# Rotary embedding on GpSimd in five instructions a tensor instead of nine

## The chip, the cores and the metric

The kernel runs on one core of a Trainium2 chip. The metric is the device time of one execution in microseconds. Five engines work side by side, each through its own list of instructions in order: TensorE (PE; its weight loads are shown apart as PEld), VectorE (DVE), ScalarE (ACT), GpSimd (POOL) and SyncE (SP), which issues most DMAs. They wait for one another by semaphores alone.

## The reference

Attention with rotary embedding over 4 batches, 8 heads, 576 positions and a head size of 64, followed by a gated feed-forward network with a convolution of three taps along the positions (512 to 1024 to 512 channels).

```python
def rotate(x):                                   # q and k
    x1, x2 = (x[..., :half], x[..., half:])
    return np.concatenate([x1 * cos - x2 * sin, x1 * sin + x2 * cos], axis=-1)
scores = scale * np.matmul(q_rot, k_rot.transpose(0, 1, 3, 2))
attn = np.exp(scores - max); attn = attn / (sum + 1e-09)
x = np.matmul(attn, v)                           # heads side by side: 512 channels
h = np.maximum(x @ w_in, 0.0)
conv_out = sum of conv_w[k] * h shifted by k - 1 positions
out = (h * sigmoid(conv_out)) @ w_out
```

## The kernel before

Two heads of one batch make a pair; there are 16 pairs. A pair takes five steps, one for each piece of 128 (the last: 64) query positions of both heads. In a step TensorE makes the scores (`sp`, L261), VectorE takes their negated maximum (`negm`, L269), ScalarE the exponential with its sum (`st`, or `str` in the last step, L273), TensorE turns the result (`tp`, L321) and ScalarE copies it out (`pt`, L199). The product with v (L389), the division by the sums (rinv, L366 to L368, and `xn`, L403) and a split of the result into a high and a low part (L406 on ScalarE, L410 on GpSimd) follow a pair later.

Beside this, the first 26 steps convert the weights of the feed-forward network, which arrive as 64-bit numbers, in pieces of 512 columns: four instructions on VectorE for each piece (L569, L575, L580, L585), a copy on ScalarE (L635) and four subtractions of 128 columns on GpSimd (L632). From step 26 on (`WIDE`) the feed-forward network itself runs between the attention steps: matmuls (L431), relu (L439), convolution on VectorE (L447, L449), tanh on ScalarE (L455), the gate (L458), a split (L466, L467), and the second product (L540, in the tail L520). After the last pair the feed-forward network goes on alone (the tail).

The rope of the pairs 1 to 15 is done by `rope` (L186 to L193) on GpSimd, once for q and once for k. The tensor `rq` or `rk` lies as 128 partitions by 18 blocks of 2 x 32 numbers. A multiplication with a table, in place (L190), covers all 1152 columns, and an addition of the second 32 numbers of each block to the first 32, in place (L193), writes 576. VectorE then turns the sums into `qT` (L234) and `kT` (L237), after which SyncE's queue loads the next pair into the same buffer (L149 to L151). Pair 0 goes another way (`rope0`, L164 to L184).

The order on every engine is written out by hand: a plan (`at(n, rank, fn)`) gives each piece of work a step and a rank in it, and inside an engine the instructions run in the order in which the plan calls them. For a pair that begins at step n, `rope` stands at step n - 6 (later pairs: n - 8 for q, n - 7 for k) with rank 18, which is at the end of a step; the transposes follow one to four steps later.

Of the kernel before, what the change touches and what calls it, by code (L numbers as in the profile page):

```python
# [12 lines left out]
ALU = mybir.AluOpType  # L13
# [7 lines left out]
def attention_moe_kernel(ctx, tc, q, k, v, w_in, conv_w, w_out, tab, tabx, out):  # L21
    nc = tc.nc
# [35 lines left out]
    tabt = keep.tile([128, S // 32, 2, 32], F32, name="tabt")  # L58
# [126 lines left out]

    def rope(p, part):  # L186
        x = raw[p, part]
        for a in range(0, 18, 3):
            y = x[:, a:a + 3]
            nc.gpsimd.tensor_tensor(out=y, in0=y, in1=tabt[:, a:a + 3], op=ALU.mult)  # L190
        for a in range(0, 18, 6):
            y = x[:, a:a + 6]
            nc.gpsimd.tensor_tensor(out=y[:, :, 0, :], in0=y[:, :, 0, :], in1=y[:, :, 1, :], op=ALU.add)  # L193

    QT, KT = {}, {}
# [502 lines left out]
    def emit():  # L698
        with tc.manual_schedule(engines=engines):
# [18 lines left out]
            for p in range(1, NP):  # L718
                n = STEPS * p
                early = n - 10 >= WIDE - 1  # L720
                for i, part in enumerate("qk"):
                    if p > 1:
                        at(max(n - 10, WIDE) if early else n - 9 + 2 * i, 19.6 if early else 19, lambda p=p, part=part: load(p, part))
                    at(n - 8 + i if early else max(n - 6, 0), 18, lambda p=p, part=part: rope(p, part))
                    at(n - 5 + i * (n - 15 < WIDE) if early else max(n - 4 + 2 * i, 2), 0.45, lambda p=p, part=part: emit_TQ(p, part))
                at(n + 1, 19, lambda p=p: load_v(p))
# [144 lines left out]
```

## Time and profile before

| What | Value |
|---|---|
| Three runs | 481.36, 483.17 and 483.62 us, median 483.17 |
| The profiled execution | span 480.6 us, 12404 instructions; the profile gives no other time for it |
| TensorE | 450.5 us busy (94%) |
| VectorE | 359.5 us busy (75%), 640 instructions |
| ScalarE | 331.9 us busy (69%) |
| GpSimd | 304.5 us busy (63%), 487 instructions |
| Granted TensorE clock | 0.996 of full speed over the span |

The busy shares are means over stages that differ: weights are converted up to some 160 us, the attention and the feed-forward network run together up to some 390 us, and the rest is feed-forward alone. A busy time counts an instruction from its start to its end, with whatever it waits for in between. The rows below take the stages apart.

### The profile page before, as it was taken

What the parts mean: (1) busy time and instruction counts of PE and PEld (TensorE: products, weight loads), DVE (VectorE), ACT (ScalarE), POOL (GpSimd) and SP (SyncE); (2) the same over time, 40 slices, a digit from 0 to 9 for tenths busy, and PEclk for the clock granted to TensorE, in tenths of its full rate; (3) what the DMA queues carried; (4) which work ended last, traced back from release to release, by engine and by line L of the source; (5) the groups of instructions that cost most, each with busy time, mean ns of one, the idle gap of its engine ahead of it and who ended that gap; (6) DMA issues with size and microseconds to landing.
All of it is one profiled execution on the core that took longest, in us unless ns stands there. A gap on an engine that the chain in (4) does not pass through costs nothing.

```text
span 480.6 us, 12404 instructions
## 1 busy us (share of the span) xinstructions
PE 450.5 (94%) x4572; PEld 355.8 (74%) x4572; DVE 359.5 (75%) x640; ACT 331.9 (69%) x951; POOL 304.5 (63%) x487
## 2 busy tenths in 40 slices
PE   1879887988999999999999999999999999999997
PEld 1446554656767787979788887879787978899886
DVE  5599899996898987777868686866874656467921
ACT  1699787887879786868778686867695953245510
POOL 3869999999797979393929394756530313144510
PEclk9999999899999999999999999999999999999999
DMA  9985877856436070718153362518020100100011
GB/s 186 245 138 158 175 179 143 152 117 161 74 81 142 9 149 25 137 37 134 39 99 74 78 95 60 103 40 145 9 66 16 49 13 25 46 22 23 0 67 44
DMA packets 140559, 42.71 MB, mean 89 GB/s; under 512 B 132156, under 2 KB 135252, under 8 KB 140500
## 3 DMA queue, kind: packets, MB, share of 16 engines
q1 hardware_dynamic: 139156, 41.54, 41.0%
q8 instruction: 36, 0.59, 0.5%
q10 hardware_dynamic: 1344, 0.39, 0.4%
q14 instruction: 23, 0.19, 0.1%
HBM read 37.12 MB, written 4.79 MB: 87 GB/s over the span
## 4 chain that ended last, share of the span: by engine, by line
PE 69%; DVE 9%; DMA 7%; SPq 7%; ACT 5%; issue 2%; POOL 0%; DVEq 0%; POOLq 0%
PE pm L431 13%; PE pm L540 11%; PE sp L261 11%; PE pm L389 11%; PE mt L520 10%; PE mt L431 7%; PE tp L321 5%; DVE negm L269 2%; DMA rd<-rt 2%; SPq L150 2%; DMA rq<-q 2%; ACT st L273 1%; ACT pt L199 1%; SPq L151 1%; DVE c L449 1%
## 5 line engine op out<-in xcount | busy, mean ns | idle before, releaser
L269 DVE TENSOR_REDUCE negm<-sp 128x1 f32<-128x576 f32 x144 | 102.5, 748 | 32.7 <-PE sp L261 24.1
L273 ACT ACTIVATE st<-sp,negm 128x576 f32<-128x576 f32 x128 | 93.7, 739 | 31.1 <-DVE negm L269 30.1
L261 PE MATMUL sp<-kT,qT 64*128 64x288 f32 (+4 forms) x556 | 98.7, 458 | 3.1 <-ACT st L273 1.3
L199 ACT ACTIVATE pt<-tp 128x512 f32<-128x512 f32 (+3 forms) x176 | 84.3, 532 | 3.7 <-PE tp L321 3.3
L449 DVE SCALAR_TENSOR_TENSOR c<-rr,cw,c 128x288 f32<-128x288 f32 x128 | 80.6, 629 | 4.2
L467 POOL TENSOR_TENSOR gm<-c,gm 128x288 fp32r<-128x288 f32 (+4 forms) x72 | 44.7, 626 | 49.7 <-ACT gm L466 49.7
L431 PE MATMUL pm<-xT,winh 128*128 128x290 f32 x352 | 74.5, 305 | 0.0
L190 POOL TENSOR_TENSOR rq<-rq,tabt 128x192 f32<-128x192 f32 x90 | 59.9, 698 | 11.7 <-DMA rq<-q 8.7
L410 POOL TENSOR_TENSOR xT<-xn,xT 128x290 fp32r<-128x290 f32 x32 | 29.5, 923 | 58.0 <-ACT xT L406 57.9
L261 PEld LDWEIGHTS sp<-kT,qT 64*128 64x128 f32 (+1 forms) x556 | 46.3, 176 | 24.2 <-issue 9.1
L321 PEld LDWEIGHTS tp<-idf,st 64*128 64x128 f32 x1024 | 42.6, 140 | 25.7 <-ACT st L273 12.9
L190 POOL TENSOR_TENSOR rk<-rk,tabt 128x192 f32<-128x192 f32 x90 | 56.9, 665 | 1.5 <-DMA rk<-k 1.1
L321 PE MATMUL tp<-idf,st 64*128 64x64 f32 x1024 | 49.4, 228 | 9.1 <-ACT st L273 7.3
L431 PEld LDWEIGHTS pm<-xT,winh 128*128 128x128 f32 x352 | 56.2, 189 | 1.8
L431 PE MATMUL pm<-xT,winl 128*128 128x290 f32 x176 | 52.0, 295 | 0.0
L389 PE MATMUL pm<-pt,vm 128*64 128x290 f32 x368 | 49.8, 411 | 0.4 <-ACT pt L199 0.4
L540 PE MATMUL pm<-wouth,gm 64*128 64x256 f32 x512 | 49.3, 281 | 0.0
L458 DVE SCALAR_TENSOR_TENSOR c<-c,rr 128x288 f32<-128x288 f32 x64 | 38.6, 624 | 10.4 <-ACT c L455 10.4
L540 PEld LDWEIGHTS pm<-wouth,gm 64*128 64x128 f32 x512 | 41.9, 185 | 0.0
L447 DVE TENSOR_SCALAR c<-rr,cw 128x288 f32<-128x288 f32 x56 | 24.9, 444 | 20.4 <-ACT rr L439 20.0
L389 PEld LDWEIGHTS pm<-pt,vm 128*64 128x64 f32 x368 | 25.6, 136 | 17.6 <-ACT pt L199 1.1
L540 PE MATMUL pm<-woutl,gm 64*128 64x256 f32 x256 | 37.7, 276 | 0.0
(118 smaller groups left out, 907.2 us busy)
## 6 DMA issues: line engine op xcount, KB each, us to landing
rq<-q SPq DMA_DIRECT2D x30, 144.0 KB
rq<-q SPq DMA_DIRECT2D x60, 72.0 KB
rk<-k SPq DMA_DIRECT2D x30, 144.0 KB
rk<-k SPq DMA_DIRECT2D x60, 72.0 KB
w<-moe_w_in SPq DMA_DIRECT2D x8, 512.0 KB
vm<-v SPq DMA_DIRECT2D x32, 128.0 KB
w<-moe_w_out SPq DMA_DIRECT2D x8, 512.0 KB
rb<-rd SPq DMA_DIRECT2D x16, 144.0 KB
```

Source lines behind the costliest of these rows:

```text
L190: nc.gpsimd.tensor_tensor(out=y, in0=y, in1=tabt[:, a:a + 3], op=ALU.mult)
L199: nc.scalar.activation(out=out, in_=in_, func=AF.Copy, scale=1.0 if sc is None else sc)
L261: nc.tensor.matmul(out=out, lhsT=qt[64 * h:64 * h + 64, c], rhs=kt[64 * h:64 * h + 64, a:a + n], start=True, stop=True)
L269: reds.setdefault((p, s), []).append(lambda: nc.vector.tensor_reduce(out=nm, in_=sc, axis=AX.XY if len(sc.shape) == 3 else AX.X, op=ALU.ma ...
L273: lambda: nc.scalar.activation(out=dst, in_=sc, func=AF.Exp, bias=nm, scale=1.0, accum_out=sm)
L321: nc.tensor.transpose(ps[r][:, 64 * k:64 * k + 64], x[i], idf[i, i])
L389: nc.tensor.matmul(out=xp[64 * h:64 * h + 64, :], lhsT=vmain[p][:, h, i, :] if i < 4 else vrem[p % 2][:, h, :], rhs=pt[:, 2 * i + h if i < ...
L431: nc.tensor.matmul(out=ps[:, 0:XW], lhsT=w[:, kk, fs], rhs=xT[:, xs, e, :], start=(i == 0), stop=(i == n - 1))
L449: nc.vector.scalar_tensor_tensor(out=c, in0=r[:, j + e:j + e + HS], scalar=cw[:, 8 * e + f:8 * e + f + 1], in1=c, op0=ALU.mult, op1=ALU.add,)
L467: nc.gpsimd.tensor_tensor(out=lo, in0=c[:, o:o + n], in1=hi.bitcast(F32), op=ALU.subtract)
L520: nc.tensor.matmul(out=ops[tt][:, 0:width], lhsT=g_tile(tt, f, e), rhs=w[:, f, cols], start=(f == 0 and i == 0), stop=(f == NF - 1 and i = ...
L540: nc.tensor.matmul(out=ps[r][:, 0:256], lhsT=g_tile(tt, f, e)[rows], rhs=w[rows, f, cols], start=(f == 0 and i == 0), stop=(f == NF - 1 an ...
```

## The change

The multiplication with the table is cut into three pieces of 384 columns instead of six of 192, and the addition into two of 288 instead of three of 192. The same numbers are computed in the same buffers. `y` now covers 6 blocks of 2 x 32 in the first loop and 9 in the second.

```diff
--- before.py
+++ after.py
@@ -185,11 +185,11 @@
 
     def rope(p, part):
         x = raw[p, part]
-        for a in range(0, 18, 3):
-            y = x[:, a:a + 3]
-            nc.gpsimd.tensor_tensor(out=y, in0=y, in1=tabt[:, a:a + 3], op=ALU.mult)
         for a in range(0, 18, 6):
             y = x[:, a:a + 6]
+            nc.gpsimd.tensor_tensor(out=y, in0=y, in1=tabt[:, a:a + 6], op=ALU.mult)
+        for a in range(0, 18, 9):
+            y = x[:, a:a + 9]
             nc.gpsimd.tensor_tensor(out=y[:, :, 0, :], in0=y[:, :, 0, :], in1=y[:, :, 1, :], op=ALU.add)
 
     QT, KT = {}, {}
```

No instruction changes its place on TensorE, VectorE, ScalarE or SyncE; on GpSimd only the rope's instructions differ. GpSimd's list around the second and third pair's ropes (`winl` are low halves of weights, `xT` the low part of an attention result), with - for before and + for after:

```order
 L632 TENSOR_TENSOR winl<-wf,winh 128x128 x12
 L410 TENSOR_TENSOR xT<-xn,xT 128x290
-L190 TENSOR_TENSOR rq<-rq,tabt 128x192 x6
-L193 TENSOR_TENSOR rq<-rq 128x6x32 x3
-L190 TENSOR_TENSOR rk<-rk,tabt 128x192 x6
-L193 TENSOR_TENSOR rk<-rk 128x6x32 x3
+L190 TENSOR_TENSOR rq<-rq,tabt 128x384 x3
+L193 TENSOR_TENSOR rq<-rq 128x9x32 x2
+L190 TENSOR_TENSOR rk<-rk,tabt 128x384 x3
+L193 TENSOR_TENSOR rk<-rk 128x9x32 x2
 L632 TENSOR_TENSOR winl<-wf,winh 128x128 x4
```

Four groups with 18 instructions become four groups with 10, between the same neighbours.

The same engine later, where TensorE is busy throughout: the ropes of one of the later pairs, first before the change (`gm` and `gb` are low parts of the gated result).

```order
L410 TENSOR_TENSOR xT<-xn,xT 128x290
L190 TENSOR_TENSOR rq<-rq,tabt 128x192 x6
L193 TENSOR_TENSOR rq<-rq 128x6x32 x3
L410 TENSOR_TENSOR xT<-xn,xT 128x290
L190 TENSOR_TENSOR rk<-rk,tabt 128x192 x6
L193 TENSOR_TENSOR rk<-rk 128x6x32 x3
L467 TENSOR_TENSOR gb<-c,gb 128x64
```

And after the change:

```order
L410 TENSOR_TENSOR xT<-xn,xT 128x290
L190 TENSOR_TENSOR rq<-rq,tabt 128x384 x3
L193 TENSOR_TENSOR rq<-rq 128x9x32 x2
L410 TENSOR_TENSOR xT<-xn,xT 128x290
L190 TENSOR_TENSOR rk<-rk,tabt 128x384 x3
L193 TENSOR_TENSOR rk<-rk 128x9x32 x2
L467 TENSOR_TENSOR gb<-c,gb 128x64
```

The xT subtraction between the two ropes, and the gm and gb subtractions behind them, stand where they stood.

## Rows read from the trace of the kernel before

**Rows 1.** Busy time by stretch: us, then busy us (instructions) of each engine.

```profile
26.00:104.00 78.00, 67.78 (x749) 43.02 (x749) 73.69 (x122) 67.23 (x178) 73.67 (x116) 0.98 0.75 155
...
121.00:160.00 39.00, 37.25 (x354) 28.07 (x352) 36.89 (x57) 33.86 (x97) 32.92 (x49) 1.00 0.45 91
160.00:343.00 183.00, 182.75 (x2160) 150.88 (x2158) 141.69 (x251) 140.99 (x412) 127.68 (x203) 1.00 0.41 80
```

**Rows 2.** What VectorE waited for, 26-104, then 121-160: us, times, longest.

```profile
DVE qT L234 <- POOL rq L193: 2.0, 3, 1.0
...
DVE c L458 <- ACT c L455: 1.1, 3, 0.6
```

**Rows 3.** Timeline, VectorE, 6 to 9 us: start, us, engine, line, operation.

```profile
6.43 0.42 DVE L183 TENSOR_TENSOR t1q<-t1q,rq 128x256 f32<-128x256 f32 x1
6.78 1.48 DVE L184 TENSOR_TENSOR t1q<-t1q,rq 128x256 f32<-128x256 f32 x1
```

**Rows 4.** Timeline, GpSimd alone at work or undisturbed, three places.

```profile
6.65 1.33 POOL L171 TENSOR_TENSOR t1k<-rk,tabs 128x512 f32<-128x512 f32 x1 [6.21 <-DMA rr<-k]
...
16.32 1.13 POOL L193 TENSOR_TENSOR rq<-rq 128x192 f32<-128x192 f32 x2
...
238.66 0.58 POOL L193 TENSOR_TENSOR rk<-rk 128x192 f32<-128x192 f32 x1
```

**Rows 5.** Timeline, GpSimd, three rope multiplications from 51.94 us.

```profile
51.94 0.59 POOL L190 TENSOR_TENSOR rq<-rq,tabt 128x192 f32<-128x192 f32 x1 [0.18 <-DMA rq<-q]
...
52.49 0.77 POOL L190 TENSOR_TENSOR rq<-rq,tabt 128x192 f32<-128x192 f32 x1
...
53.22 1.04 POOL L190 TENSOR_TENSOR rq<-rq,tabt 128x192 f32<-128x192 f32 x1
```

**Rows 6.** Timeline, VectorE, the same stretch.

```profile
52.08 0.73 DVE L575 TENSOR_SCALAR wt<-wt 128x512 int32<-128x512 int32 x1
52.85 0.96 DVE L580 SCALAR_TENSOR_TENSOR wt<-w,wt 128x512 int32<-128x512 int32 x1
53.73 0.56 DVE L366 TENSOR_SCALAR rvc<-sums 128x9 f32<-128x9 f32 x1
...
56.01 1.01 DVE L585 SCALAR_TENSOR_TENSOR wf<-w,wt 128x512 int32<-128x512 int32 x1
```

**Rows 7.** Busy time of line 190 (26-104, 121-160), of line 193 (26-104).

```profile
26.00:104.00 78.00, 31.88 (x48) 0.98 0.75 155
...
121.00:160.00 39.00, 12.25 (x18) 1.00 0.45 91
...
26.00:104.00 78.00, 15.42 (x23) 0.98 0.75 155
```

**Rows 8.** VectorE groups, 26-104: count, then busy us, mean ns, idle before.

```profile
L585 DVE SCALAR_TENSOR_TENSOR wf<-w,wt 128x512 int32<-128x512 int32 x11 | 9.8, 894 | 0.4
L580 DVE SCALAR_TENSOR_TENSOR wt<-w,wt 128x512 int32<-128x512 int32 x11 | 9.5, 863 | 0.2
L569 DVE TENSOR_SCALAR wt<-wt 128x512 f32<-128x512 f32 x11 | 7.8, 712 | 0.0
L575 DVE TENSOR_SCALAR wt<-wt 128x512 int32<-128x512 int32 x11 | 6.6, 604 | 0.2
```

**Rows 9.** By line: ns min/median/max, first and last start, forms.

```profile
L569 DVE TENSOR_SCALAR wt<-wt x17: 417/677/1018, 20.1 to 152.3; 128x512 f32<-128x512 f32 x16, 32x128 f32<-32x128 f32 x1
...
L580 DVE SCALAR_TENSOR_TENSOR wt<-w,wt x16: 684/926/1175, 21.3 to 157.6; 128x512 int32<-128x512 int32 x16
...
L366 DVE TENSOR_SCALAR rvc<-sums x16: 125/554/767, 35.1 to 391.7; 128x9 f32<-128x9 f32 x16
```

**Rows 10.** Timeline, one TensorE-bound step: VectorE, ScalarE, TensorE.

```profile
255.22 1.50 DVE L449 SCALAR_TENSOR_TENSOR c<-rr,cw,c 128x288 f32<-128x288 f32 x2
...
257.64 0.74 ACT L273 ACTIVATE str<-sp,negm 128x576 f32<-128x576 f32 x1
...
260.22 1.13 PE L261 MATMUL sp<-kT,qT 64*128 64x288 f32 x8
```

## The prediction

> **What bounds the kernel now.** I read the busy time by stretch first, cut where the binding engine changes [rows 1]. From 160 to 343 us TensorE is busy for 182.75 of 183 us; it sets the pace and the others fit in beside it. From 26 to 104 us it is busy for 67.78 of 78 us only. There two other engines are nearly full: VectorE (DVE) with 73.69 and GpSimd (POOL), which does the rope, with 73.67. From 121 to 160 us VectorE has 36.89 of 39. The reader is to see that two engines at 94% can't both be read as the bound, since a busy time holds the waits inside an instruction too. So the second view is what VectorE waits for between instructions [rows 2]: from 26 to 104 us it is 2.0 us in three waits for the rope of q, from 121 to 160 us 1.1 us behind the tanh on ScalarE. VectorE runs almost without a gap, in program order, and whatever lengthens its instructions there lengthens the stretch.
>
> The third view says what is inside those instructions. The subtraction L183 and the addition L184 have the same shape, 128x256. L183 took 0.42 us; L184, begun at 6.78, took 1.48 and ended at 8.26 [rows 3]. POOL ran one 512-column instruction from 6.65 to 7.98 [rows 4]. So a VectorE instruction with two operands in SBUF stood still until the POOL instruction had ended, and needed another 0.28 us after it. The same holds the other way round: of the three rope instructions 128x192 from 51.94 on, the undisturbed one took 0.59, the next 0.77 and the third 1.04 [rows 5], while VectorE's L575 and L580 took their turns between them [rows 6]. The two engines take turns, whole instructions at a time.
>
> **The change part by part.** Nothing moves on any engine; 270 POOL instructions of 192 columns become 90 of 384 and 60 of 288.
>
> What POOL saves. Two additions of 192 columns back to back take 1.13 us, one alone 0.58, so the pitch is 0.55; the one of 512 columns took 1.33 [rows 4]. That is (1.33 - 0.58) / 320 = 2.34 ns a column, and 0.55 - 192 x 0.00234 = 0.10 us for each instruction besides. Estimated from these, a 384 lasts 1.03 us with a pitch of 1.00, and a 288 lasts 0.80 with 0.775. A rope goes from 9 x 0.55 = 4.95 to 3 x 1.00 + 2 x 0.775 = 4.55 us, 0.40 us less. From 26 to 104 us there are 48 multiplications of 192, eight ropes; from 121 to 160 us 18, three ropes [rows 7]. That is 3.2 and 1.2 us of POOL time. It counts only where someone waits for POOL: the 2.0 us of [rows 2]. I take all of that as gained, which is the most that these waits hold.
>
> What VectorE pays. From 26 to 104 us the four kinds of weight conversion have 11 instructions each with means of 0.894 and 0.863 (L585, L580), 0.712 and 0.604 us (L569, L575) [rows 8]; undisturbed they take 0.684 and 0.417 (the minima of L580 and L569; L585 and L575 have the same size) [rows 9]. So 11 x (0.210 + 0.179 + 0.295 + 0.187) = 9.6 us is waiting, 0.22 us each. The six of L403 and four of L366 at the same 0.22 bring it to 11.8. Rope holds 31.88 + 15.42 = 47.3 of POOL's 73.67 busy us there [rows 1, 7], 64%, so 7.5 us of waiting stand behind rope, 0.157 us for each of its 48 multiplications. From 121 to 160 us there are 18: 2.8 us.
>
> By how much this grows is not shown by a row, so I bound it. If VectorE's instructions arrive at random, the waiting goes with the sum of the squared pitches: (3 x 1.00² + 2 x 0.775²) / (9 x 0.55²) = 1.54. If they come in a row, each must sit out a whole further POOL instruction. I read one stretch that way, row by row [rows 5, 6]. Before, L575, L580, L366 and L585 take 0.73 + 0.96 + 0.56 + 1.01 = 3.26 us; without waits, with the minima 0.42, 0.68, 0.68 and 0.13 us for L366, 1.91: the waiting is 1.35. After, the first 384 ends at 52.97 and L575 0.28 later (as it did after the 52.53 of before), at 53.25: 1.17. The next 384, held up 0.18 by L575, ends at 54.14, and L580 0.55 later: 1.40. The third, held up 0.45, ends at 55.58, L366 just after it: 0.87. What stands between L366 and L585 takes 1.72 as before (54.29 to 56.01); both additions are done by 57.1, the rope of k begins, L585 (from 57.3) sits out its first 384 and takes 1.33. Sum 4.77, waiting 2.86, a factor of 2.1. In return the wait of the next instruction, qT's transpose, for POOL (the longest of [rows 2], 1.0 us) is gone. I take 1.8, midway, because not all stretches are packed like this one.
>
> The sum: 26 to 104 us, 0.8 x 7.5 = 6.0, less 2.0: +4.0. From 121 to 160 us, 0.8 x 2.8 = 2.2, less the 1.1 us of idle time that can take it up: +1.1. From 160 to 343 us: nothing. There five conv instructions of one step, the last ending at 256.72, are followed by a reduction, by its exponential on ScalarE from 257.64 to 258.38, and by the score matmuls that need its buffer at 260.22 [rows 10]: 1.84 us of cover. Stepped through in the same way, with each of the five behind a longer POOL instruction, they end 1.4 us later. If that cover is gone, TensorE pays (below). Before 26 us VectorE waits for weights to land, and five such meetings at 0.157 are 0.8 us at most: 0 in the sum, kept for the upper end. Together +5.1 us on the span of 480.6. The times shown have a median of 483.17, 2.6 above that span; I carry the difference over: 488.3. The lower end (1.54, everything given back) is 4.1 - 2.0 + 1.5 - 1.1 = +2.5, 485.7; the upper (2.1, nothing given back) 8.2 + 3.1 + 0.8 = +12.1, 495.3.
>
> A rule that bears on this: the Trainium skill, SBUF — State Buffer, section "SBUF: two separate sides", states that VectorE with two SBUF inputs and GpSimd share one port pair, that whichever starts first has it for its whole instruction, and that the other fully blocks. [Rows 3, 4] agree (1.48 us against 0.42). By the rule alone an instruction that comes just behind the start of a 384 would lose its whole 1.03 us.
>
> A rule that speaks for the change: the Trainium skill, GPSIMD Engine Reference, section 2.1 "Instruction dispatch", puts tens of cycles of dispatch on each GpSimd instruction. The 0.10 us an instruction of [rows 4] agrees in kind; by the rule alone the change can only gain.
>
> **The rivals.**
> Faster: POOL is the real pace-setter from 26 to 160 us. For it: POOL is as busy as VectorE, and VectorE does wait for rope three times. Against it: part of POOL's busy time is VectorE's turns (0.77 and 1.04 us where 0.59 would do). It decides if VectorE's waiting grows by a factor under 1.27, since then 0.27 x 7.5 us are no more than the 2.0 us gained. Price: between -2.0 (481.2) and all of POOL's 3.2 + 1.2 = -4.4 (478.8); I take 480.5.
> No change: VectorE waits longer but the 2.0 us at qT, the 1.1 us at the tanh, and less rope for it to meet cancel it; the lower end with another 2.5 us of slack found, for instance where loads and not VectorE release the next step. 483.2. Against it: VectorE has no other idle time of that size in those stretches.
> Slower still: the cover in the TensorE-bound part fails, in the step at 253 to 260 us and its like, one per 26 us, seven in all. If each is overrun by 1 us, +7 on top of the +5.1: 495.3. It decides where the delay passes 1.84 us; for it speaks that the 1.4 us worked out above come near to that.
>
> **How the numbers follow.** My forecast (+2.5 to +12.1 us) has 0.57, the slower rival 0.13, no change 0.17, faster 0.13. About 0.5% (2.4 us) is what a measurement of this kernel can tell from no change. Faster by more: 0.13. Within: 0.17. Slower: 0.70. The likeliest case's own range is 485.5 to 494; for 8 in 10 I take 482 to 496, which leaves out most of the faster case and the worst of the slower one.
>
> **What would show it.** L190 near 1.0 us and L193 near 0.80 where undisturbed, a rope 0.4 us shorter. From 26 to 104 us the means of L569, L575, L580 and L585 higher by 0.1 to 0.3 us, no waits of qT for POOL, and the stretch that ends at 104 ending some 4 us later; POOL less busy. The steps from 160 us on should keep their period. The forecast is wrong if these means stay (no whole-instruction turns, or VectorE is served first), if they rise and TensorE's bound part starts no later (the slack was elsewhere), or if the period from 160 us on grows.

## The result, and the profile after

The changed kernel takes 488.7 us (median of 7 runs, 487.78 to 491.70), the kernel before 483.62 (median of 7). The ratio is 1.0112, with a 95% interval of 1.0086 to 1.0138: slower, by some 5.1 us (medians). The forecast was 488.3.

The profiled execution after is the longest of the seven, with a span of 489.6 us; the other six have spans of 485.7 to 487.1. So about 3 of the 9.0 us between the two traces are this execution's own, and about 1 more is there because the trace of before (480.6) is of a fast one; its median span is 481.5. Two stretches of the trace after have a lower granted clock of TensorE (the third number from the right), 0.86 of full speed, where the trace of before has 0.93 and 1.00:

```profile
75.00:100.00 25.00, 20.21 (x201) 12.98 (x203) 21.45 (x34) 17.67 (x48) 21.16 (x27) 0.86 0.67 129
150.00:175.00 25.00, 23.46 (x199) 17.64 (x198) 22.81 (x33) 19.61 (x57) 20.02 (x25) 0.86 0.38 73
```

The clock has two levels, 1.2 and 2.4 GHz. At the lower one the same sixteen matmuls take nearly twice as long, which shows in the first of these stretches (start, us, engine, line, operation; the row of the stretch is from 86.1 to 92.9 us):

```profile
82.42 1.21 PE L389 MATMUL sp<-pt,vm 128*64 128x145 f32 x16
...
90.28 2.20 PE L389 MATMUL sp<-pt,vm 128*64 128x145 f32 x16
...
86.10:92.90 6.80, 6.18 (x46) 4.06 (x46) 4.91 (x10) 4.40 (x11) 6.23 (x13) 0.50 0.90 196
```

Just before, TensorE had stood for 1.1 and 1.4 us, waiting for ScalarE and VectorE. At an equal granted clock the result stands. Three of the seven executions have a mean granted clock of 0.996, with spans of 485.7 to 486.7 us; fifteen executions of the kernel before have the same 0.996, with spans of 479.7 to 483.1 and a mean of 481.1. The difference is 5 us there too. Whether the change makes the clock fall more often is open. But what single stretches of a trace lose has to be read with their clock beside it.

Below I take from the trace after times before 150 us, and lengths of steps. For shifts I also use the trace with the longer pieces in pairs 1 to 8 alone (span 486.6), whose instructions up to 150 us are those of the changed kernel. Its granted clock is 0.92 from 27 to 111 us, lower than in the trace after (0.96) and in that of before (0.98) there.

The rope's instructions, by line (ns min/median/max, first and last start):

```profile
L190 POOL TENSOR_TENSOR rq<-rq,tabt x45: 993/1180/1452, 13.6 to 341.0; 128x384 f32<-128x384 f32 x45
...
L193 POOL TENSOR_TENSOR rq<-rq x30: 778/856/1241, 16.5 to 342.9; 128x288 f32<-128x288 f32 x30
```

Undisturbed, a 384 takes 0.99 us and a 288 0.78, against 1.03 and 0.80 expected from [rows 4]. But the median multiplication is 1.18 us, a whole turn of VectorE longer.

The stretch of [rows 5] and [rows 6], the ropes of pair 3 (those of the first listing of the change), first GpSimd (start, us, engine, line, operation):

```profile
53.72 1.18 POOL L190 TENSOR_TENSOR rq<-rq,tabt 128x384 f32<-128x384 f32 x1
...
54.86 1.18 POOL L190 TENSOR_TENSOR rq<-rq,tabt 128x384 f32<-128x384 f32 x1
...
56.01 1.24 POOL L193 TENSOR_TENSOR rq<-rq 128x288 f32<-128x288 f32 x1
...
60.76 2.14 POOL L190 TENSOR_TENSOR rk<-rk,tabt 128x384 f32<-128x384 f32 x2 [2.75 <-DMA rd<-rt]
```

and VectorE:

```profile
54.08 1.10 DVE L575 TENSOR_SCALAR wt<-wt 128x512 int32<-128x512 int32 x1
55.22 1.37 DVE L580 SCALAR_TENSOR_TENSOR wt<-w,wt 128x512 int32<-128x512 int32 x1
56.51 0.76 DVE L366 TENSOR_SCALAR rvc<-sums 128x9 f32<-128x9 f32 x1
...
58.99 0.68 DVE L585 SCALAR_TENSOR_TENSOR wf<-w,wt 128x512 int32<-128x512 int32 x1
59.59 0.77 DVE L234 STREAM_TRANSPOSE qT<-rq 128x576 f32<-128x576 f32 x1
```

L575 now ends 0.28 us behind the POOL instruction that ends at 54.90, and L580 0.55 behind the one that ends at 56.04: the same turns, longer. The first three take 3.23 us where 2.25 did. L585 meets nobody, because the rope of k waits 2.75 us for a transfer (the profile names `rd<-rt`); and L234 no longer waits for POOL.

Busy time by stretch (span of the stretch; PE, PEld, DVE, ACT, POOL; clock, DMA share, GB/s). The first two rows, before and after, hold the same instructions of VectorE, from the reduction at 26.34 us before to the last ahead of the L575 at 104.42; the third is from the trace after:

```profile
26.34:104.42 78.08, 67.86 (x752) 43.17 (x750) 73.74 (x123) 67.31 (x178) 74.09 (x117) 0.98 0.75 156
...
27.21:110.68 83.47, 69.68 (x760) 44.16 (x760) 78.77 (x123) 68.07 (x179) 71.32 (x91) 0.96 0.70 147
...
169.00:352.00 183.00, 183.00 (x2166) 151.35 (x2164) 152.95 (x250) 141.02 (x412) 115.86 (x139) 1.00 0.41 80
```

VectorE is busy for 78.77 us with what took 73.74, 5.0 us more; its idle time is 83.47 - 78.77 = 4.7 us, against 4.3 before. POOL is busy 71.32, 2.8 less in a stretch that is 5.4 us longer. From 169 to 352 us, the stretch that began at 160 in [rows 1], VectorE has 152.95 us of work for 141.69, and TensorE still needs 183.

Conversion by conversion in the first stretch, to be held against [rows 8] (count | busy us, mean ns | idle before):

```profile
L580 DVE SCALAR_TENSOR_TENSOR wt<-w,wt 128x512 int32<-128x512 int32 x11 | 11.5, 1042 | 0.2
L585 DVE SCALAR_TENSOR_TENSOR wf<-w,wt 128x512 int32<-128x512 int32 x11 | 9.8, 891 | 0.4
L575 DVE TENSOR_SCALAR wt<-wt 128x512 int32<-128x512 int32 x11 | 8.6, 777 | 0.2
L569 DVE TENSOR_SCALAR wt<-wt 128x512 f32<-128x512 f32 x10 | 7.4, 744 | 0.0
```

L580 and L575 pay some 0.18 us each, L569 0.03, L585 nothing. So two of the four means that were to rise did so. What VectorE waits for between its instructions, 26 to 110 us:

```profile
DVE negm L269 <- PE sp L389: 1.9, 1, 1.9
DVE xn L403 <- DMA rk<-k: 1.2, 1, 1.2
```

The 2.0 us of waiting for the rope of q are gone, as forecast; other waits, of 3.1 us in these two rows, stand in their place. The longer of them, from 91.1 to 93.0 us, ends with the stretch at half clock that is shown above:

```profile
93.03 0.76 DVE L269 TENSOR_REDUCE negm<-sp 128x1 f32<-128x576 f32 x1 [1.95 <-PE sp L389]
```

### The profile page after: what moved, and what is told of

It reads as the page before. It is cut to its first block, busy times and chain, and to the rows that moved or that the text cites. A ratio compares the mean times of both kernels' runs of the same rounds, so it can differ in the third digit from the quotient of the medians.

```text
span 489.6 us, 12284 instructions
## 1 busy us (share of the span) xinstructions
PE 453.3 (93%) x4572; PEld 357.9 (73%) x4572; DVE 379.8 (78%) x640; ACT 332.4 (68%) x951; POOL 284.6 (58%) x367
## 4 chain that ended last, share of the span: by engine, by line
PE 70%; DVE 12%; DMA 6%; SPq 5%; ACT 4%; issue 2%; ACTq 0%; DVEq 0%
PE pm L431 14%; PE sp L261 12%; PE pm L389 11%; PE pm L540 11%; PE mt L520 10%; PE mt L431 7%; PE tp L321 5%; DVE negm L269 4%; DMA rq<-q 2%; ACT st L273 2%; SPq L150 1%; DMA rd<-rt 1%; DVE wt L580 1%; DVE wt L569 1%; DVE c L449 1%
## 5 line engine op out<-in xcount | busy, mean ns | idle before, releaser
L269 DVE TENSOR_REDUCE negm<-sp 128x1 f32<-128x576 f32 x144 | 102.3, 747 | 33.8 <-PE sp L261 24.9
L261 PE MATMUL sp<-kT,qT 64*128 64x288 f32 (+4 forms) x556 | 100.1, 463 | 4.4 <-ACT str L273 1.5
L449 DVE SCALAR_TENSOR_TENSOR c<-rr,cw,c 128x288 f32<-128x288 f32 x128 | 89.4, 698 | 4.2
L467 POOL TENSOR_TENSOR gm<-c,gm 128x288 fp32r<-128x288 f32 (+4 forms) x72 | 47.7, 666 | 58.7 <-ACT gm L466 58.7
L431 PE MATMUL pm<-xT,winh 128*128 128x290 f32 x352 | 75.5, 308 | 0.0
L410 POOL TENSOR_TENSOR xT<-xn,xT 128x290 fp32r<-128x290 f32 x32 | 28.5, 892 | 67.8 <-ACT xT L406 67.7
L261 PEld LDWEIGHTS sp<-kT,qT 64*128 64x128 f32 (+1 forms) x556 | 46.6, 178 | 26.4 <-issue 10.4
L190 POOL TENSOR_TENSOR rq<-rq,tabt 128x384 f32<-128x384 f32 x45 | 50.1, 1141 | 13.6 <-DMA rq<-q 9.2
L190 POOL TENSOR_TENSOR rk<-rk,tabt 128x384 f32<-128x384 f32 x45 | 51.0, 1160 | 4.7 <-DMA rd<-rt 3.4
L458 DVE SCALAR_TENSOR_TENSOR c<-c,rr 128x288 f32<-128x288 f32 x64 | 44.5, 716 | 9.8 <-ACT c L455 9.8
L447 DVE TENSOR_SCALAR c<-rr,cw 128x288 f32<-128x288 f32 x56 | 27.3, 488 | 19.1 <-ACT rr L439 18.8
L455 ACT ACTIVATE c<-c 128x288 f32<-128x288 f32 x64 | 28.5, 445 | 15.6 <-DVE c L449 15.6
```

Of the source, the lines that this page charges most:

```text
L190: nc.gpsimd.tensor_tensor(out=y, in0=y, in1=tabt[:, a:a + 6], op=ALU.mult)
L261: nc.tensor.matmul(out=out, lhsT=qt[64 * h:64 * h + 64, c], rhs=kt[64 * h:64 * h + 64, a:a + n], start=True, stop=True)
L269: reds.setdefault((p, s), []).append(lambda: nc.vector.tensor_reduce(out=nm, in_=sc, axis=AX.XY if len(sc.shape) == 3 else AX.X, op=ALU.ma ...
L431: nc.tensor.matmul(out=ps[:, 0:XW], lhsT=w[:, kk, fs], rhs=xT[:, xs, e, :], start=(i == 0), stop=(i == n - 1))
L449: nc.vector.scalar_tensor_tensor(out=c, in0=r[:, j + e:j + e + HS], scalar=cw[:, 8 * e + f:8 * e + f + 1], in1=c, op0=ALU.mult, op1=ALU.add,)
L467: nc.gpsimd.tensor_tensor(out=lo, in0=c[:, o:o + n], in1=hi.bitcast(F32), op=ALU.subtract)
```

## The experiments

The kernel before was run beside each; ratios are to it.

**Where the cost arises.** The longer pieces in some pairs only:

```diff
+        m, s = (6, 9) if p <= 8 else (3, 6)      # the second kernel: if p > 8
-        for a in range(0, 18, 3):  ...           # multiplication: pieces of m blocks
-        for a in range(0, 18, 6):  ...           # addition: pieces of s blocks
```

Pairs 1 to 8:

> The longer pieces for pairs 1 to 8 alone, whose ropes ran before 163 us. Theory A (VectorE pays where it is the bound, nothing where TensorE is): the whole cost, +5 us on the kernel before, +3 to +7. Rival B (every rope with long pieces costs the same, wherever it runs): 8 of 15 pairs, +2.7 us. Rival C (the cost comes where TensorE is the bound, because its cover fails): +0 to +1.

Measured: 1.0102 (1.0063 to 1.0142), 488.4 us. Pairs 9 to 15:

> The longer pieces for pairs 9 to 15 alone, whose ropes ran from 176 us on. Theory A: no change, within 1 us of the kernel before, though VectorE's L449 and L458 get longer by some 0.1 to 0.2 us in the mean there. Rival B (same cost for each rope): 7 of 15 pairs, +2.4 us. Rival C (the cover fails in the TensorE-bound part): +4 to +5.

Measured: 1.0016 (0.9985 to 1.0047), no change that can be told. So the whole cost, as far as can be told, comes from the ropes up to 163 us. C falls clearly, B narrowly: its +2.7 and +2.4 us lie just outside the two intervals (3.0 to 6.9, and -0.7 to 2.3 us). That the later ropes do cost VectorE something, and that it is covered, the second kernel's rows from 176 to 343 us show, those of before first:

```profile
176.00:343.00 167.00, 167.00 (x1981) 137.67 (x1982) 126.07 (x224) 127.62 (x376) 114.70 (x183) 1.00 0.42 81
```

```profile
176.00:343.00 167.00, 167.00 (x1988) 138.14 (x1985) 138.36 (x224) 128.00 (x377) 106.89 (x126) 1.00 0.43 81
```

As many VectorE instructions (224) take 138.36 us, not 126.07: 12.3 us more, over twice what the first 110 us cost, and TensorE is at 167.00 of 167 both times.

In the trace of the first kernel (one line is added in it, so L270 is L269 and L262 is L261) the reduction that began at 110.49 before begins at 116.04:

```profile
116.04 0.75 DVE L270 TENSOR_REDUCE negm<-sp 128x1 f32<-128x576 f32 x1
```

and the score matmuls of [rows 10], at 260.22 before, begin at 266.30:

```profile
266.30 1.13 PE L262 MATMUL sp<-kT,qT 64*128 64x288 f32 x8
```

+5.6 us by 110 us and +0.5 us from there to TensorE's part, all in all +6.1 in this execution. The +5.6 hold what the clock of 0.92 cost there.

**Multiplication or addition.** Only one of the two loops with longer pieces:

```diff
-        for a in range(0, 18, 3):   # multiplication, in the first kernel
+        for a in range(0, 18, 6):
-        for a in range(0, 18, 6):   # addition, in the second kernel
+        for a in range(0, 18, 9):
```

> The multiplication in three pieces of 384, the addition still in three of 192. Theory A by the squares of the pitches: 3 x 1.00² + 3 x 0.55² against 9 x 0.55² is a factor of 1.44 of the 1.54 for both, so four fifths of VectorE's extra waiting, and three of the four saved POOL instructions: about +4 us, +2.5 to +6. Rival D (what counts is how often VectorE and POOL change turns, not how long a turn is): fewer instructions mean fewer turns, so no cost: 0 or less.

Measured: 1.0081 (1.0054 to 1.0109), 3.9 us by the ratio.

> The addition in two pieces of 288, the multiplication still in six of 192. Theory A: a factor of (6 x 0.55² + 2 x 0.775²) / (9 x 0.55²) = 1.11, so a fifth of the extra waiting: about +1 us, 0 to +2. Rival D (number of turns): 0 or less. A sum of this run and the one with the multiplication alone that is far from the whole change would say that the two don't add.

Measured: 1.0028 (1.0004 to 1.0052), 1.4 us by the ratio. Both grow, in about the proportion of the squared pitches, and 3.9 + 1.4 = 5.3 is the whole change (5.4 by its ratio). D falls: fewer turns did not help.

The traces of these two have the full clock all through the first stretch. The same instructions of VectorE as above, with the longer multiplication, then with the longer addition:

```profile
26.78:106.09 79.31, 66.72 (x762) 42.59 (x760) 77.70 (x122) 68.01 (x178) 71.22 (x95) 1.00 0.76 154
...
27.04:106.48 79.44, 66.50 (x752) 42.27 (x752) 74.94 (x122) 67.50 (x177) 72.98 (x110) 1.00 0.77 156
```

VectorE is busy 4.0 and 1.2 us longer than the 73.74 of before, together 5.2, where the whole change has 5.0. Its idle time is 1.6 us with the longer multiplication and 4.5 with the longer addition, against 4.3 before.

**Longer still, and shorter.** The two loops with steps of 9 and 18 blocks (576 columns), of 2 and 3 (128 and 96), and of 1 and 2 (64 columns each):

```diff
-        for a in range(0, 18, 3):   # multiplication
+        for a in range(0, 18, 9):   # 2 and 1 in the other two kernels
-        for a in range(0, 18, 6):   # addition
+        for a in range(0, 18, 18):  # 3 and 2
```

> Two multiplications of 576 columns and one addition of 576 for each rope: the same cost pushed further. A 576 has a pitch of 1.45 us by 2.34 ns a column; a rope takes 4.35 us of POOL, 0.60 less than before. Theory A: the squares give 3 x 1.45² / (9 x 0.55²) = 2.3, VectorE waits 13 us more, less what the waits for POOL give back and what the smaller number of meetings takes off: +7 to +11 us on the kernel before. Rival D (the number of turns counts): 0 or less. If the cost stops growing at +5, the price of a meeting does not follow the length of the POOL instruction.

Measured: 1.0447 (1.0411 to 1.0484), 21.6 us: the direction of A, and twice its size. Part of the rest is what the prediction had as its slower rival. Here the cover in TensorE's part fails; TensorE's waits from 160 to 343 us, where the kernel before has 0.2 us in all:

```profile
PE sp L261 <- ACT str L273: 3.5, 6, 1.0
PE pm L389 <- ACT pt L199: 3.1, 1, 3.1
```

Six score matmuls wait for the exponential whose cover [rows 10] shows. Some of the remainder can be the clock's: from 26 to 104 us it is 0.86 to 0.88 in this trace, against 0.98 before. How much, no run shows.

> Nine multiplications of 128 columns and six additions of 96 for each rope. By the trace of before a 128 has a pitch of 0.40 and a 96 of 0.325 us: a rope takes 9 x 0.40 + 6 x 0.325 = 5.55 us of POOL, 0.60 more. Theory A: the squares give a factor of 0.76, so VectorE waits some 2.5 us less up to 160 us, against waits of qT for POOL that grow by up to the 0.6 us of each of eight ropes: between -2.5 and +2, likeliest -1. Rival E (POOL sets the pace up to 160 us, and the cost of the change came from something else): 11 ropes by 0.60, +6.6 us.

Measured: 1.0475 (1.0421 to 1.0528), 23 us. A and E both missed this by far. What A says of VectorE is so: in the first stretch it is busy for 70.86 us, 2.9 less than before. But its idle time grows from 4.3 to 12.8 us.

> Eighteen multiplications of 64 columns and nine additions of 64 for each rope. A 64 has a pitch of 0.25 us: a rope takes 27 x 0.25 = 6.75 us of POOL, 1.8 more than before. Theory A alone (turns of whole instructions, POOL never the bound) gives a factor of 27 x 0.25² / (9 x 0.55²) = 0.62, -3 to -4 us. But POOL was busy 73.67 of 78 us from 26 to 104 us, and eight ropes bring it 14 us more, so POOL is late and VectorE waits for the end of each rope: I expect that this outweighs it, +3 to +8 us.

Measured: 1.1503 (1.1458 to 1.1547), 73 us. In the direction expected, but some ten times the size. With 128 and 96 columns, GpSimd's busy time from 104 to 160 us (the fifth pair of numbers) fills the stretch:

```profile
104.00:160.00 56.00, 49.17 (x470) 36.55 (x470) 45.68 (x81) 44.76 (x125) 56.00 (x110) 0.97 0.58 119
```

and VectorE waits for rope's end, over the whole span:

```profile
DVE kT L237 <- POOL rk L193: 24.0, 12, 4.2
...
DVE qT L234 <- POOL rq L193: 7.6, 4, 2.8
```

Most of the loss of the kernel with 128 and 96 columns arises in TensorE's part: a reduction is 6.9 us later than before at 200 us, 15.3 at 324. There VectorE waits for kT five times, 16.2 us in all (207 to 362 us). Then one instruction adds 8.7 us at a stroke. It takes 0.36 us undisturbed:

```profile
351.56 9.27 DVE L447 TENSOR_SCALAR c<-rr,cw 128x288 f32<-128x288 f32 x1 [2.25 <-ACT rr L439]
```

GpSimd runs one instruction behind the other in that time, up to 360.66 us, and L447 ends at 360.83. So the turns are not always one instruction each: here VectorE was passed over until GpSimd stopped. I had priced the added instructions at 0.10 us each, when GpSimd is undisturbed. But the mean ones are longer than the undisturbed (128 columns, 0.45 us), by my reading because each further instruction gives VectorE one more chance to go first:

```profile
L190 POOL TENSOR_TENSOR rq<-rq,tabt 128x128 f32<-128x128 f32 x135 | 68.6, 544 | 13.6 <-DMA rq<-q 13.5
L190 POOL TENSOR_TENSOR rk<-rk,tabt 128x128 f32<-128x128 f32 x135 | 65.3, 520 | 0.0
L193 POOL TENSOR_TENSOR rq<-rq 128x96 f32<-128x96 f32 x90 | 36.7, 441 | 0.0
L193 POOL TENSOR_TENSOR rk<-rk 128x96 f32<-128x96 f32 x90 | 36.3, 437 | 0.0
```

These four sum to 206.9 us for 30 ropes; before, L190 and L193 had 59.9 + 56.9 + 30.0 + 29.8 = 176.6 by the same view. That is 1.0 us a rope, not the 0.60 I added up, and GpSimd had no slack for it. So on this side the faster rival's mechanism (GpSimd sets the pace) is true. The kernel before lies between two slopes, and none of the other cuts of the rope that were run beats it.

**Is VectorE's waiting on the path at all?** The rope left out:

```diff
-        (both loops of rope)
+        y = x[:, 17:18]
+        nc.gpsimd.tensor_tensor(out=y[:, :, 0, :], in0=y[:, :, 0, :], in1=y[:, :, 1, :], op=ALU.add)
```

> Leaves out the rope of pairs 1 to 15 but for one addition of 32 columns each, which keeps the order of the waits. Theory A: VectorE's 10.3 us of waiting behind rope up to 160 us and the 2.0 us of waiting for rope's end go: -8 to -12 us on the kernel before. Rival F (VectorE's waits inside its instructions are slack up to 160 us; loads or other engines set the pace): 0 to -3 us.

Measured: 0.9839 (0.9788 to 0.9889), 7.8 us less: just short of the range, and no slack as F had it. I take it as an estimate of the most that any better cut of this rope could gain.

This kernel also shows how much of VectorE's relief is lost on the way. In the first stretch VectorE is busy for 62.64 us, 11.1 less than before, but the stretch is only 5.1 us shorter (73.02 us), at the same clock of 0.98: VectorE now waits longer for TensorE's matmuls instead.

```profile
DVE negm L265 <- PE sp L385: 4.7, 8, 1.1
```

That VectorE is freer here does not by itself say which engine was the limit, since GpSimd has less to do as well. The memsets below keep GpSimd busy.

**Is it the rope in particular?** The weights' low parts, another GpSimd job, in one piece of 512 columns:

```diff
-                for o in range(0, 512, 128):
-                    w = slice(o, o + 128)
+                for o in range(0, 512, 512):
+                    w = slice(o, o + 512)
```

> The rope as before; the low parts of the weights (L632) in one POOL instruction of 512 columns for each piece, not in four of 128. POOL is spared 3 x 0.10 us for each of 16 pieces, 4.8 us in all. Theory A holds for any POOL instruction that VectorE meets: a 512 lasts 1.33 us with a pitch of 1.30, and 1.30² / (4 x 0.40²) = 2.6; L632 has 22.3 of POOL's 73.67 busy us from 26 to 104 us, so some 3.6 of 11.8 us of VectorE's waiting there: +5.7 us gross, +3 to +6 with what POOL's earlier end gives back. Rival G (the cost is particular to the rope, its in-place operands or its place in the step): 0, or a small gain from POOL's 4.8 us.

Measured: 1.0068 (1.0028 to 1.0108), 3.3 us. So a long GpSimd instruction outside the rope costs time too, and G falls. In its trace VectorE is busy 79.35 us in the first stretch, 5.6 more than before, where +5.7 gross was forecast. That execution is the longest of its ten; it holds another VectorE instruction that was passed over, beside a rope in its old cut (undisturbed 0.42 us), and the last GpSimd instruction of that run:

```profile
122.39 5.18 DVE L569 TENSOR_SCALAR wt<-wt 128x512 f32<-128x512 f32 x1
...
126.47 0.82 POOL L410 TENSOR_TENSOR xT<-xn,xT 128x290 fp32r<-128x290 f32 x1
```

L569 ends at 127.57, again 0.28 us behind it.

**Must the GpSimd instruction read?** Memsets in place of the rope:

```diff
-        (both loops of rope)
+        for a in range(5):
+            nc.gpsimd.memset(x, 0.0)
```

> Leaves out the rope of pairs 1 to 15: in its place POOL sets the whole tile to zero five times, in five instructions that write 1152 columns and read nothing, so POOL is busy in the same places. Theory A1 (VectorE's instructions with two operands in SBUF wait only for POOL instructions that read SBUF): L580, L585, L449 and L458 come down to near their minima behind these, and the time falls by 4 to 8 us against the kernel before, as most of it does with no rope at all. Theory A2 (any POOL instruction makes them wait for its end): they wait as behind the rope, and the time stays within 3 us of the kernel before, or above it if one such instruction takes over 1 us.

Measured: 0.9931 (0.9901 to 0.9960), 3.3 us less, between A1 and A2, and the groups say why. VectorE from 26 to 104 us (the lines stand four lower here: L571 is L575, L565 L569, L581 L585, L576 L580):

```profile
L571 DVE TENSOR_SCALAR wt<-wt 128x512 int32<-128x512 int32 x11 | 10.2, 925 | 0.2
L565 DVE TENSOR_SCALAR wt<-wt 128x512 f32<-128x512 f32 x11 | 8.7, 789 | 0.0
L581 DVE SCALAR_TENSOR_TENSOR wf<-w,wt 128x512 int32<-128x512 int32 x11 | 8.6, 778 | 0.4
L576 DVE SCALAR_TENSOR_TENSOR wt<-w,wt 128x512 int32<-128x512 int32 x11 | 8.2, 745 | 0.2
```

The two with two operands in SBUF are near their minimum of 0.684 us, though memsets of 1.09 us run beside them; the two with one operand, at half the time for the same size, wait longer than behind the rope (0.604 and 0.712 in [rows 8]). By line (ns min/median/max), against 684/926/1175 for L580 in [rows 9]:

```profile
L571 DVE TENSOR_SCALAR wt<-wt x17: 424/1240/1245, 20.5 to 150.7; 128x512 int32<-128x512 int32 x16, 32x128 int32<-32x128 int32 x1
...
L576 DVE SCALAR_TENSOR_TENSOR wt<-w,wt x16: 651/692/968, 21.7 to 154.6; 128x512 int32<-128x512 int32 x16
```

So A1 is right about the instructions with two operands. In the first stretch nothing is gained, since the others wait longer (77.82 us, 78.08 before). The 3.3 us come from the stretch that took 39.13 us from 121.15 on and takes 35.83 here, where the convolution (L449, here L445) has two operands:

```profile
L449 DVE SCALAR_TENSOR_TENSOR c<-rr,cw,c 128x288 f32<-128x288 f32 x14 | 11.2, 798 | 0.2
...
L445 DVE SCALAR_TENSOR_TENSOR c<-rr,cw,c 128x288 f32<-128x288 f32 x14 | 7.7, 549 | 0.2
```

GpSimd is as full as before there (31.80 us of 35.83, 33.05 of 39.13), so it is VectorE's relief, and not GpSimd's, that goes with the shorter stretch. The engines are said above to wait for one another by semaphores alone; these waits inside instructions come on top of that.

## Why the prediction was right, step by step

What bounds the kernel. Right. The ropes up to 163 us carry the cost, and those behind it none that can be told. That VectorE's inner waits are on the path the memsets show (3.3 us less, with GpSimd as busy), and the kernel without rope agrees (7.8 us less).

What VectorE pays. Right in mechanism and nearly in size from 26 to 104 us: +5.0 us of busy time for the same instructions, where 0.8 x 7.5 = 6.0 was forecast. It fell on L575 and L580 rather than on all four. In the stretch read row by row, the first three instructions came to 1.10, 1.37 and 0.76 us against 1.17, 1.40 and 0.87; the fourth, forecast at 1.33, took 0.68. That one was mis-sized because GpSimd stood still for 2.75 us there, waiting for a transfer, and VectorE did not meet it. In the whole stretch GpSimd waits 6.0 us for transfers, 3.4 before; why, no run shows.

What POOL gives back. This term can't be settled from the trace after. I took all of the 2.0 us of waits for the rope of q as gained. They did go, but VectorE's idle time in that stretch went from 4.3 to 4.7 us. Of the waits in their place, 1.95 us stand behind matmuls at half clock: the sixteen took 2.20 us, not 1.21, and the eight score matmuls in front of them 2.18, not 1.19 as at 64.58 us. That is 2.0 us, so I estimate that at the full clock this wait would not have been there. With the longer multiplication alone and the full clock, the idle time fell from 4.3 to 1.6 us, by more than the 2.0 that the forecast has for the whole change.

From 121 to 160 us I forecast +1.1, out of 2.2 us more work for VectorE. This is not confirmed. VectorE's busy time for the same instructions there, 37.17 us before, is 36.43 in the trace with the long pieces up to pair 8 and 40.13 in the trace after, whose clock is 0.92 there. The first has +0.5 us from 110 us to TensorE's part. So in that execution the part up to 110 us came out 1.6 us higher than the +4.0 forecast, at a clock of 0.92, and this one 0.6 lower. That the sum came so near (5.1 us, 5.1 forecast) is partly luck.

From 160 to 343 us. Right: the step keeps its length. The five conv instructions of [rows 10] were forecast to end 1.4 us later within the step; in the trace after, where that step begins 9.0 us later, they end at 266.84, 1.1 later than 256.72 + 9.0:

```profile
264.93 1.91 DVE L449 SCALAR_TENSOR_TENSOR c<-rr,cw,c 128x288 f32<-128x288 f32 x2
```

The exponential then starts at 267.54, 0.9 later in the step, and TensorE's matmuls at 269.24, exactly 9.0 later than 260.22.

The rivals. The faster one (GpSimd sets the pace) is wrong for this change, since GpSimd was busy 2.8 us less in the first stretch and the time rose, but true for shorter pieces. The slower one (the cover fails) did not occur here, and did with 576 columns. Both bounds that I gave for the growth came from squares and back-to-back turns; taken over the whole first stretch, and put down to the rope alone, 5.0 us more on 7.5 is a factor of 1.67, between the 1.54 and the 2.1. Neither bound reckons with a VectorE instruction that is passed over by several GpSimd instructions.

The two rules of the Trainium skill that were weighed: SBUF — State Buffer, "SBUF: two separate sides", agrees, and the memsets show its clause that a VectorE instruction with two SBUF inputs is held only by a GpSimd instruction that reads SBUF (0.745 us beside 1.09 us memsets). GPSIMD Engine Reference, "Instruction dispatch", speaks of GpSimd's own time; there the trace agrees (2.8 us less busy in the first stretch with fewer instructions), but it was the smaller effect, and the rival that goes by this rule alone is wrong here.

## What to carry to other kernels

Where VectorE is the bound and GpSimd works beside it in SBUF, read VectorE's inner waits (mean against minimum of one line) before its idle time: a GpSimd instruction's length is what VectorE pays at each meeting, and its count is what GpSimd pays. The best length lies between, and is to be looked for in the stage where VectorE sets the pace; where TensorE does, long pieces are free until a step's cover is used up. A gain priced at the wait that it removes is an upper bound, as in the kernel without rope, where 11.1 us less of VectorE made the first stretch 5.1 us shorter: ask which wait is due next. And before a wait in one trace is put down to a change, look at the granted clock of the same few microseconds.

## What was not expected of the hardware

VectorE and GpSimd mostly take turns, but not always: VectorE instructions of under half a microsecond stood for 9.27 us (128 and 96 columns), 6.35 us (64 columns) and 5.18 us (weights' low parts in one piece) while GpSimd ran instruction after instruction, and went on only when GpSimd stopped. No VectorE instruction took over 1.86 us in the trace of before, or over 1.5 us in the trace after. What decides it, no run shows.

Cutting GpSimd's work finer cost it much more than the undisturbed pitch says: 1.0 us a rope for six more instructions, not 0.60, and 73 us in all with 27 instructions of 64 columns a rope. A GpSimd memset did not hold up VectorE's instructions with two SBUF operands, but did hold up those with one (0.93 against 0.42 us undisturbed).
